# Residual rows through DRAM in place of TensorE, an MLP in groups of 256 rows, and a new order of steps

## The chip, the cores and the metric

One core of one Trainium2 chip runs the kernel. The metric is the device time of one execution in microseconds (us). The engines are TensorE (PE; its weight loads are PEld), VectorE (DVE), ScalarE (ACT), GpSimd (POOL) and SyncE (SP). POOL, SP and ACT issue DMAs.

## The reference

Inputs are q, k, v (4 batches, 8 heads, 768 rows, 64 columns, float32), `sort_net` (4, 8, 8, 8) and the MLP weights (512 x 2048 and 2048 x 512). In short:

```python
P = sinkhorn(sort_net)                 # 5 rounds of exp, row and column normalisation
k_sorted = einsum('bhij,bhjcd->bhicd', P, k_blocks)    # 8 blocks of 96 rows; v the same
attn = softmax(q_block @ k_sorted_block.T / 8)         # within each block
x = (attn @ v_sorted_block), heads side by side        # (4, 768, 512)
u = x + real(fft(fft(x, axis=1), axis=2))
un = (u - mean(u)) / sqrt(var(u) + 1e-6)               # over the 512 columns
out = u + relu(un @ w_ch1) @ w_ch2
```

## The kernel before

The program works batch by batch (b = 0 to 3 in the code, **batches 1 to 4** here), with two batches in flight: the attention of one batch overlaps the MLP of the one before. Nothing is left to a scheduler. The code declares some 1,300 steps (`step`, or `chain` for steps that follow each other), each with a name, a batch, the engines that may run it, what it reads and writes. `Plan.ORDER`, a long list of step numbers, gives the order in which they are issued, with a letter where an engine other than the first is taken. Each engine runs its own steps strictly in that order; a step that waits holds all behind it on its engine. Buffers come from rings of fixed size (`ring`), PSUM from eight banks.

Stages of a batch, with the step names that the prediction uses:

- `mix`: kron products of P (`make_kron`), mixed q, k, v on TensorE (`psQK`, `psV`), block means `a16`.
- attention: `psS` (scores), `max`, `exp`, `minus` (the exponentials less one, so that the means carry the constant part; in batches 3 and 4 in halves of four blocks, tile `es`), `turn_e` (transposed by a DMA on SP into `eT`), `psN` (values) and `norm`, which writes normalised values to `xr` (97 or 99 partitions, 8 blocks, 512 columns). The block means are kept apart and put into extra rows of `xr` by DMAs on SP (`a_out`, L634; `row_zero`, L642).
- Fourier transform: `fold`, `psWe`, `psWo` over the rows, `psF` over the columns, giving `PQ`.
- residual (`residual`): 6 tiles of 128 rows per batch, numbered by (i, m), i = 0 to 2, m = 0 or 1 for mirrored rows. A selection matrix `rsel` picks the 128 rows of x, in the order of the spectrum, out of `xr` on TensorE (L978; two matmuls of 512 columns, for i = 1 two of half the width). In batch 1 VectorE adds this to `PQ` straight from PSUM; in batches 2 to 4 it is copied to `u` (L431 on ACT, L435 on VectorE) and POOL adds `PQ` (`add_res`, L990, L991).
- normalisation: `stats` (L1005, L1006), `root` (L1014, L1015), `nm` (L1018), `normal` (L1028 on ACT, L1031 on VectorE), `transpose_u` (on SP by DMA, L1043; in batch 1 on TensorE).
- `mlp`: groups of three tiles (384 rows): 16 first-stage pieces of four matmuls (L1070) with a relu on ACT each (L1076), then 12 second-stage pieces of four matmuls (L1088), an evacuation on VectorE (L1097) into `outt`, and a store: an indirect scatter on POOL (L1109), for the last two tiles plain DMAs on SP and ACT (L1105).

POOL also issues the loads of k, q, v and weights (L443, L453, L1119, L1123). Most are throttled: POOL first copies one element of an earlier load (`landed`, L377), which waits until that has landed.

## Time and profile before

| | |
|---|---|
| median of 3 runs | 293.38 us (292.58 to 295.56) |
| profiled execution | 293.0 us, span 290.8 us, mean granted TensorE clock 0.992 |
| PE busy | 271.7 us (93%), 2581 matmuls |
| PEld, DVE, ACT, POOL busy | 160.5, 194.5, 175.2, 125.1 us |
| DMA | 30.40 MB, mean 105 GB/s |

The span runs from the first to the last instruction. Busy time is the sum of instruction durations on an engine. Matmuls overlap in TensorE's pipeline, so its busy time counts somewhat more than the pace at which it works through its queue.

### The profile page before, as it was taken

How to read it: one execution, taken by the hardware profiler on the slowest of the kernel's cores; microseconds unless marked ns; L12 is line 12 of the kernel's file. 1: busy time of each engine (PE TensorE's matmuls, PEld its weight loads, DVE VectorE, ACT ScalarE, POOL GpSimd, SP SyncE). 2: the span in 40 equal slices, each digit the busy share in tenths (PEclk: the TensorE clock that was granted, in tenths of full speed). 3: DMA queues.
4: the chain of work that ended last, by engine and by line, in shares of the span. 5: the costliest groups of instructions: out<-in, count | busy, mean ns of one | idle time of the engine just before them, and what ended most of it. 6: DMA issues, size and time to landing. Idle time of an engine off the chain costs nothing.

```text
span 290.8 us, 6800 instructions
## 1 busy us (share of the span) xinstructions
PE 271.7 (93%) x2581; PEld 160.5 (55%) x2581; DVE 194.5 (67%) x446; ACT 175.2 (60%) x444; POOL 125.1 (43%) x192
## 2 busy tenths in 40 slices
PE   6799899899969999979999899999999999999994
PEld 2466667556735566436656566455555555545541
DVE  6778989998868758657977887886575744211011
ACT  2268875878917776667775889969422660532520
POOL 8769596254527657689005117311010634211110
PEclk9989999999999999999999999999999999999999
DMA  7999949979964991895926622443310103312102
GB/s 100 182 217 192 184 66 180 215 114 139 151 95 70 140 152 41 145 160 113 136 54 126 134 60 66 103 108 92 79 37 18 38 18 109 78 42 80 38 36 72
DMA packets 50481, 30.40 MB, mean 105 GB/s; under 512 B 25851, under 2 KB 48587, under 8 KB 50448
## 3 DMA queue, kind: packets, MB, share of 16 engines
q0 software_dynamic: 19344, 20.48, 40.8%
q1 hardware_dynamic: 30906, 9.20, 16.2%
q8 instruction: 20, 0.33, 0.5%
q10 hardware_dynamic: 200, 0.30, 0.3%
q14 instruction: 11, 0.09, 0.1%
HBM read 28.50 MB, written 6.29 MB: 120 GB/s over the span
## 4 chain that ended last, share of the span: by engine, by line
PE 57%; DMA 19%; DVE 7%; ACT 6%; issue 4%; POOL 4%; SPq 0%; ACTq 0%; POOLq 0%; DVEq 0%
PE bank L1070 23%; PE bank L1088 20%; DMA w1sb<-in_moe_w_ch_dram 5%; DMA w2sb<-in_moe_w_ch_dram 5%; DMA unT<-un 4%; DMA eT<-es 4%; PE bank L978 2%; PE bank L935 2%; DMA v<-in_v_dram 2%; ACT sm L782 2%; ACT sm L770 1%; PE bank L873 1%; DVE mns L788 1%; PE bank L651 1%; POOL q L453 1%
## 5 line engine op out<-in xcount | busy, mean ns | idle before, releaser
L1070 PE MATMUL bank<-unT,w1sb 128*128 128x384 f16 x512 | 90.0, 326 | 3.6 <-DMA unT<-un 3.0
L1088 PE MATMUL bank<-w2sb,hr 128*128 128x512 f16 x384 | 88.0, 379 | 2.2 <-DMA w2sb<-in_moe_w_ch_dram 2.2
L1076 ACT ACTIVATE hr<-bank 128x384 f16<-128x384 f32 x128 | 56.5, 495 | 44.2 <-PE bank L1070 42.9
L1070 PEld LDWEIGHTS <-w1sb 128*128 128x128 f16 x512 | 48.3, 98 | 36.0 <-DMA unT<-un 3.8
L1088 PEld LDWEIGHTS <-hr 128*128 128x128 f16 x384 | 36.5, 98 | 42.9 <-issue 2.7
L1109 POOL DMA_INDIRECT out_dram<-outt,idx_sb x22 | 22.1, 1006 | 86.3 <-DVE outt L1097 61.0
L1097 DVE SCALAR_TENSOR_TENSOR outt<-u,bank 128x512 f32<-128x512 f32 x24 | 16.4, 682 | 41.8 <-PE bank L1088 35.6
L782 ACT ACTIVATE sm<-bank,mns 96x96 f32<-96x96 f32 x128 | 31.0, 348 | 6.5 <-DVE mns L788 6.4
L990 POOL TENSOR_TENSOR u<-u,PQ 128x257 f32<-128x257 f32 x18 | 12.3, 684 | 32.2 <-DVE PQ L948 25.5
L431 ACT CAST W<-bank 128x384 f16<-128x384 f32 (+1 forms) x36 | 11.8, 387 | 19.0 <-PE bank L895 9.8
L834 DVE TENSOR_TENSOR xr<-bank,rz 96x512 f16<-96x512 f32 x32 | 22.0, 687 | 1.1
L788 DVE TENSOR_REDUCE mns<-bank 96x8 f32<-96x768 f32 x16 | 14.9, 949 | 4.6 <-PE bank L743 4.1
L1005 DVE BATCH_NORM_STATS2 st<-u 128x6 f32<-128x512 f32 x24 | 16.4, 684 | 0.2
L753 DVE TENSOR_REDUCE mxs<-bank 96x8 f16<-96x768 f32 x16 | 14.8, 948 | 2.0 <-PE bank L743 2.0
L662 DVE SCALAR_TENSOR_TENSOR vo<-a,bank 128x384 f16<-128x384 f16 x24 | 12.6, 546 | 3.3 <-PE bank L651 2.9
L827 PEld LDWEIGHTS <-eT 97*128 97x128 f16 (+1 forms) x256 | 11.5, 101 | 5.8 <-DMA eT<-es 1.1
L827 PE MATMUL bank<-vs,eT 97*128 97x65 f16 (+1 forms) x256 | 12.9, 196 | 1.8 <-DMA eT<-es 0.5
L770 ACT ACTIVATE sm<-bank 96x768 f32<-96x768 f32 x16 | 12.9, 803 | 2.7 <-PE bank L743 1.8
L443 POOL DMA_DIRECT2D v<-in_v_dram x16 | 11.7, 730 | 3.9 <-PE bank L654 2.3
L873 PE MATMUL bank<-cso_sb,xso 120*128 120x384 f16 (+1 forms) x64 | 12.9, 326 | 0.2 <-DVE amt L599 0.2
L833 DVE RECIPROCAL rz<-bank 96x8 f32<-96x8 f32 x32 | 6.3, 197 | 9.8 <-PE bank L827 7.5
L798 ACT ACTIVATE es<-sm 96x384 f16<-96x384 f32 x21 | 11.1, 527 | 2.6 <-DMA eT<-es 1.3
(150 smaller groups left out, 425.4 us busy)
## 6 DMA issues: line engine op xcount, KB each, us to landing
vs<-vo SPq DMA_DIRECT2D x48, 65.0 KB
v<-in_v_dram POOLq DMA_DIRECT2D x16, 192.0 KB, 4.9
k<-in_k_dram POOLq DMA_DIRECT2D x15, 192.0 KB, 4.7
q<-in_q_dram POOLq DMA_DIRECT2D x15, 192.0 KB, 4.9
w1sb<-in_moe_w_ch_dram POOLq DMA_DIRECT2D x4, 512.0 KB, 10.2
w2sb<-in_moe_w_ch_dram POOLq DMA_DIRECT2D x4, 512.0 KB, 7.0
eT<-es SPq DMA_TRANSPOSE x32
cdh_sb<-cdh POOLq DMA_DIRECT2D x1, 387.0 KB, 4.1
```

Source lines behind the costliest of these rows:

```text
L770: ("exp", b, {"A": 810}, lambda e: nc.scalar.activation(sms[n].t.rearrange("p (t j) c -> p t (j c)", t=2), pS.t[0:BLK, :, 0:4 * BLK], AF.Exp),
L782: nc.scalar.activation(sm.t[:, i], pair(pS, BLK)[:, t, i % 4], AF.Exp, bias=mn.t[:, i:i + 1], scale=-1.0)
L788: ("max", b, {"V": 945}, lambda e: nc.vector.tensor_reduce(mn.t.rearrange("p (t j) -> p t j", t=2), pair(pS, BLK), axis=AX.X, op=ALU.min), ...
L827: nc.tensor.matmul(ps[0:wide(i).stop - BLK * i, i // 4, i % 4], et[0:97, wide(i)], vs[b % 2][:, 4 * y + i % 4, (D + 1) * h:(D + 1) * (h + 1)])
L834: nc.vector.tensor_tensor(xr2[b % 2][0:BLK, 4 * y:4 * y + 4, 128 * hp:128 * hp + 128].rearrange("p j (t d) -> p t j d", t=2), ps[:, :, :, ...
L873: nc.tensor.matmul(ps, x[0:n, j], cso[0:n, j, :], start=(j == 0), stop=(j == 3))
L1005: nc.vector.bn_stats(st.t, us[b, i, m].t)
L1070: nc.tensor.matmul(ps, w1sb[:, mc, 128 * fc:128 * fc + 128], unT[b, gr].t[:, mc, :], start=(mc == 0), stop=(mc == 3))
L1076: nc.scalar.activation(dst, bank(pH, [128, 384]), AF.Relu)
L1088: nc.tensor.matmul(ps, hr[f4].t[:, fc % 4, 128 * t:128 * (t + 1)], w2sb[:, fc, :], start=(fc == 0), stop=(fc == 15))
L1097: step("outt", b, {"V": 687}, lambda e, u=u, pC=pC, o=o: nc.vector.scalar_tensor_tensor(o.t, u.t, RSC, bank(pC, [128, DM]), op0=ALU.mult, ...
L1109: step("store", b, {"G": 1050}, lambda e: nc.gpsimd.indirect_dma_start(out=out.rearrange("b s m -> (b s) m"), out_offset=bass.IndirectOffs ...
```

## The change

In batches 2 to 4 the residual rows no longer pass TensorE. Two DRAM buffers `xd` of 768 rows by 512 columns in float16 take turns. SP first fills one with the block means, repeated (`fill`, new L993). Once all normalised values of a batch stand in `xr`, POOL adds them onto it with one accumulating DMA (`spill`, new L999). Then for each of the 6 tiles POOL gathers 128 rows by index into `xg` (`gather`, new L1006; the index has six columns more) and adds `PQ` to them, giving `u` (`add`, L988, L989). The residual matmuls, the copies of `u`, `a_out` and `row_zero` go for these batches; batch 1 keeps them.

The MLP works on groups of two tiles (one i, 256 rows). A first-stage piece is eight matmuls of 256 columns into one bank with one relu; a batch has 24 of them (32 before) and 24 second-stage pieces as before. The output is evacuated into `u` itself, so `outt` goes. Buffers: three `hr` of [128, 8, 256], three `unT` of [128, 4, 256], three `xg`. POOL may now take the halves of `minus` and the normalisation `un`. Six more warming matmuls stand in the Sinkhorn part, and `ORDER` is new throughout.

```diff
-    idx = np.concatenate([tok + S * b for b in range(B)], 1)
+    kept = NB * np.argsort(PERM)[tok % BLK] + tok // BLK
+    idx = np.concatenate([tok + S * b for b in range(B)] + [kept], 1)
...
     ORDER = """
-        0 39 1 2 3 8 9 28 29A 12 19 15 5 41 4 40V 37 38A 7 6 42V 10V 169V 53 54A 51 52A 26 81 27A 11 88 89 13 16 95 96
+        14 16 15 0 1 8 39 2 3 4 9 40V 10V 168G 28 29A 37 38A 26 27A 5 53 54A 6 7 57 55 13 11 58A 56A 51 52V 59 60 88
...
-    ring("hr", 4, [128, 4, 384], F16)
+    ring("hr", 3, [128, 8, 256], F16)
...
-    ring("unT", 2, [128, 4, 384], F16)
-    ring("outt", 2, [128, DM], F32)
+    ring("unT", 3, [128, 4, 256], F16)
+    ring("xg", 3, [128, DM], F16)
...
+    rows = ctx.enter_context(tc.tile_pool(name="rows", bufs=1, space=bass.MemoryType.DRAM))
+    xd2 = [rows.tile([S, DM], F16, name=f"xd{i}") for i in range(2)]
...
-            step("minus", b, {"V": 385, "A": 518}, g, r=[(sm, t)], w=[es])
+            step("minus", b, {"V": 360, "A": 520, "G": 850}, g, r=[(sm, t)], w=[es])
...
-            ("u", b, {"A": 585, "V": 685}, lambda e: copy(e, us[b, i, m].t, bank(pR, [128, DM])),
-             [pR], [us[b, i, m]]) if b else
             ("u", b, {"V": 730}, lambda e: add(e, us[b, i, m].t, bank(pR, [128, DM]), PQ[b, i], m),
...
-        step("add", b, {"G": 1340}, lambda e: add(e, u.t, u.t, pq, m), r=[(pq, 0), (pq, 1), u], w=[u])
+    def means_out(b):
+        xd = xd2[b % 2]
+        step("fill", b, {"S": 650}, lambda e: nc.sync.dma_start(
+            xd.rearrange("(g p) m -> p g m", g=G), a16[:, None, :].broadcast_to([128, G, DM])),
+            r=["a16"], w=[("xd", b % 2)], work=2000, hop=1600)
+
+    def rows_out(b):
+        xd, xr = xd2[b % 2], xr2[b % 2]
+        step("spill", b, {"G": 950}, lambda e: nc.gpsimd.dma_start(
+            xd.rearrange("(k i) m -> k (i m)", i=NB), xr[0:BLK].rearrange("k i m -> k (i m)"),
+            max_dma_last_dim=4096, accum_op=ALU.add),
+            r=[("x", b % 2, h, y) for h in range(H) for y in range(2)], w=[("xd", b % 2)], work=2500, hop=2200)
+
+    def rows_in(b, i, m):
+        us[b, i, m], pq, xg, t = Buf("u"), PQ[b, i], Buf("xg"), 6 * B + TILE[i, m]
+        step("gather", b, {"G": 1050}, lambda e: nc.gpsimd.indirect_dma_start(
+            out=xg.t, out_offset=None, in_=xd2[b % 2],
+            in_offset=bass.IndirectOffsetOnAxis(ap=idx[:, t:t + 1], axis=0)),
+            r=[("xd", b % 2), "idx"], w=[xg], work=500, hop=1500)
+        step("add", b, {"G": 1340}, lambda e: add(e, us[b, i, m].t, xg.t, pq, m),
+             r=[(pq, 0), (pq, 1), xg], w=[us[b, i, m]])
...
-        step("un", b, {"V": 545, "A": 814}, f,
+        step("un", b, {"V": 545, "A": 814, "G": 1130}, f,
...
+    def mlp(b, i):
+        h = [Buf("hr") for _ in range(2)]
+        MLP = 1e6 + 1e4 * b + 3e3 * i
+        for y in range(8):
             pH = Buf("bank")
...
+            def f(e, y=y, pH=pH):
+                ps = bank(pH, [128, 2, 256])
+                for x in range(2):
+                    fc = 2 * y + x
+                    for mc in range(4):
+                        nc.tensor.matmul(ps[:, x], w1sb[:, mc, 128 * fc:128 * fc + 128],
+                                         unT[b, i].t[:, mc, :], start=(x == 0 and mc == 0), stop=(mc == 3),
+                                         skip_group_check=True)
...
+            step("outt", b, {"V": 687}, lambda e, u=u, pC=pC: nc.vector.scalar_tensor_tensor(
+                u.t, u.t, RSC, bank(pC, [128, DM]), op0=ALU.mult, op1=ALU.add),
+                [pC, u], [u], prio=MLP - 1e8)
...
-            warm(7)
+            warm(12)
...
-    warm(2)
+    warm(3)
...
-        for gr in range(2):
-            mlp(b, gr)
+        for i in range(3):
+            mlp(b, i)
```

The order of instructions on an engine can be printed from the programs; a row is a line, the operation, output and inputs with buffer numbers, and the output's shape. On POOL before the change, where the last residual tile of batch 3 and the first of batch 4 get their `PQ` added, with stores between them:

```order
L1109 DMA out_dram<-outt_142,idx_sb 3072x512
L990 TENSOR_TENSOR u_117<-u_117,PQ_115 128x257
L991 TENSOR_TENSOR u_117<-u_117,PQ_115 128x255
L1109 DMA out_dram<-outt_143,idx_sb 3072x512
L1109 DMA out_dram<-outt_142,idx_sb 3072x512 x2
L990 TENSOR_TENSOR u_122<-u_122,PQ_114 128x257
L991 TENSOR_TENSOR u_122<-u_122,PQ_114 128x255
```

And on POOL of the changed kernel, from the spill of batch 4 on (L999 the spill, L1006 gathers, L1117 stores of earlier batches, L988 and L989 adds, L1045 a normalisation):

```order
L999 DMA xd_189<-xr_185 96x2x2048
L1006 DMA xg_144<-xd_189,idx_sb 128x512
L1117 DMA out_dram<-u_116,idx_sb 3072x512
L1006 DMA xg_143<-xd_189,idx_sb 128x512
L1117 DMA out_dram<-u_120,idx_sb 3072x512
L988 TENSOR_TENSOR u_122<-xg_144,PQ_113 128x257
L989 TENSOR_TENSOR u_122<-xg_144,PQ_113 128x255
L988 TENSOR_TENSOR u_116<-xg_143,PQ_113 128x257
L989 TENSOR_TENSOR u_116<-xg_143,PQ_113 128x255
L1006 DMA xg_142<-xd_189,idx_sb 128x512
L1117 DMA out_dram<-u_118,idx_sb 3072x512
L1006 DMA xg_144<-xd_189,idx_sb 128x512
```

An add needed only PSUM copies before; now it stands behind a gather, which stands behind the spill, with stores between them.

In batch 2 the same chain stands among the throttled loads. POOL of the changed kernel there, from the third gather on (L374 the `landed` copies, L451 and L441 loads):

```order
L1006 DMA xg_144<-xd_189,idx_sb 128x512
L374 COPY landed<-k_71 1x1
L451 DMA q_73<-in_q_dram 128x2x384
L988 TENSOR_TENSOR u_121<-xg_142,PQ_113 128x257
L989 TENSOR_TENSOR u_121<-xg_142,PQ_113 128x255
L374 COPY landed<-k_70 1x1
L441 DMA v_79<-in_v_dram 128x2x384
L1006 DMA xg_142<-xd_189,idx_sb 128x512
```

Between spill and third add there are loads that each wait for an earlier one; before, adds and loads also shared this queue, but no gather.

On TensorE, between the transforms of batch 4 (L895) and second-stage pieces of the MLP (L1088), before the change (L978 the residual matmuls):

```order
L1088 LDWEIGHTS hr_66
L1088 MATMUL bank<-w2sb,hr_66 128x512
L978 LDWEIGHTS rsel_sb
L978 MATMUL bank<-xr_184,rsel_sb 128x512
L978 LDWEIGHTS rsel_sb
L978 MATMUL bank<-xr_184,rsel_sb 128x512
L895 LDWEIGHTS xse
L895 MATMUL bank<-cse_sb,xse 128x194
```

And in the changed kernel, at the end of the same transforms, where the second-stage pieces (now L1100) follow at once:

```order
L895 LDWEIGHTS xse
L895 MATMUL bank<-cse_sb,xse 128x192
L895 LDWEIGHTS xse
L895 MATMUL bank<-cse_sb,xse 128x192
L1100 LDWEIGHTS hr_66
L1100 MATMUL bank<-w2sb,hr_66 128x512
```

The residual matmuls are out of the queue. From the last values of batch 4 to its first MLP matmul, TensorE of the changed kernel has 14 second-stage and 12 first-stage pieces of batch 3 (the latter of eight matmuls), and the transforms of batch 4 but for the last `psF`; for batch 3 and batch 2 some more of the like (29.2 and 37.5 us of pieces at the pace that the prediction derives).

194 lines of the change are left out of this document (89 added, 105 removed), and 3 rows, old and new, of the table ORDER.

## The prediction

> **What bounds the kernel now.** First the page's totals and its chain that ended last (shares of the span), then the table by stage (start:end, length, busy time and instruction counts of PE, PEld, DVE, ACT and POOL, granted clock, DMA share, GB/s).
>
> ```profile
> span 290.8 us, 6800 instructions
> PE 271.7 (93%) x2581; PEld 160.5 (55%) x2581; DVE 194.5 (67%) x446; ACT 175.2 (60%) x444; POOL 125.1 (43%) x192
> PE 57%; DMA 19%; DVE 7%; ACT 6%; issue 4%; POOL 4%; SPq 0%; ACTq 0%; POOLq 0%; DVEq 0%
> 40.00:60.00 20.00, 18.28 (x267) 12.84 (x265) 19.66 (x46) 14.32 (x29) 10.59 (x14) 1.00 1.12 178
> 100.00:120.00 20.00, 20.00 (x181) 12.13 (x180) 13.94 (x30) 15.23 (x38) 13.08 (x21) 1.00 0.70 113
> 200.00:220.00 20.00, 19.92 (x140) 11.26 (x139) 13.60 (x36) 7.78 (x21) 0.97 (x1) 1.00 0.24 54
> 240.00:260.00 20.00, 20.00 (x110) 10.58 (x109) 5.72 (x12) 7.38 (x19) 5.63 (x8) 1.00 0.28 80
> ```
>
> From 100 us on TensorE never rests for long and the other engines have room: what is taken from its queue there comes off the end. Between 40 and 60 us VectorE is 98% busy and DMA is loaded throughout: there TensorE waits for others now and then. Its waits, by its timeline, with the releaser behind the arrow:
>
> ```profile
> 12.08 0.27 PE L1193 MATMUL bank<-ident,pw 32*64 32x32 f32 x2 [1.62 <-DVE pw L1163]
> 57.62 0.61 PE L1052 MATMUL bank<-ident,un 128*128 128x128 f16 x8 [1.15 <-DVE qT L435]
> 85.73 1.02 PE L1088 MATMUL bank<-w2sb,hr 128*128 128x512 f16 x4 [1.25 <-DMA w2sb<-in_moe_w_ch_dram]
> 129.90 0.34 PE L1070 MATMUL bank<-unT,w1sb 128*128 128x384 f16 x1 [2.10 <-DMA unT<-un]
> 162.63 0.82 PE L1070 MATMUL bank<-unT,w1sb 128*128 128x384 f16 x4 [0.91 <-DMA unT<-un]
> ```
>
> The last two are the start of an MLP that waits for transposed rows, 3.0 us together. The changed part lies just ahead of those rows, so this is the wait to watch.
>
> **The change part by part.** TensorE first. The chain's pieces (start, length, line, matmuls) give the pace of one queue position better than the busy column, which counts the pipeline's overlap twice:
>
> ```profile
> 103.83 0.43 PE bank L978 x2
> 171.05 0.55 PE bank L978 x4
> 112.02 1.30 PE bank L1070 x8
> 180.44 0.86 PE bank L1088 x4
> 213.47 0.34 PE bank L895 x4
> 136.96 0.43 PE bank L827 x8
> ```
>
> *Residual matmuls.* Of 24 residual tiles 18 go: 12 with two full matmuls, 0.43 us each, and 6 with two half-width ones, about 0.25 (half of 0.55, less the drain of the last): 12 x 0.43 + 6 x 0.25 = 6.7 us less.
>
> *MLP in groups of 256.* The second stage keeps its 384 matmuls. The first had 512 of 384 columns at 1.30/8 = 0.1625; it gets 768 of 256. From 0.1625 (384 columns) and 0.86/4 = 0.215 (512), a column costs 0.41 ns and a matmul 5 ns, so one of 256 costs 0.110: 768 x 0.110 - 512 x 0.1625 = 84.5 - 83.2, 1.3 us more at most; by 0.34/4 = 0.085 for 193 columns it is 0.111, the same. A weight load takes 98 ns in its own rows, near 110, but the L827 matmuls with their own weight loads follow each other every 0.43/8 = 0.054, so the loads stay covered. The fewer, larger relu instructions run beside this. I take 0.7, since the two lengths are read to 0.01 us. TensorE: **-6.0 us**.
>
> *The early part.* These copies and POOL's present work stand in the groups (busy, mean ns of one):
>
> ```profile
> L431 ACT COPY u<-bank 128x512 f32<-128x512 f32 x10 | 6.0, 597 | 2.0 <-PE bank L978 2.0
> L435 DVE COPY u<-bank 128x512 f32<-128x512 f32 x8 | 5.5, 685 | 3.1 <-PE bank L978 2.8
> L1031 DVE TENSOR_SCALAR un<-u,mv,rstd 128x512 f16<-128x512 f32 x14 | 7.6, 549 | 0.0
> L510 POOL TENSOR_TENSOR kron<-pcs,small_sb 128x512 f16<-128x512 f32 x4 | 4.3, 1085 | 6.1 <-PE bank L711 6.0
> L814 POOL TENSOR_SCALAR eT<-sm 96x768 f16<-96x768 f32 x1 | 2.1, 2132 | 3.7 <-ACT sm L770 3.7
> ```
>
> Both copies go, and the new order puts the two remaining kron products of the later batches, ten half-tiles of exp minus one and nine normalisations on POOL. VectorE loses 5.5 us of copies, and three normalisations of batch 1 (3 x 0.549 = 1.6) around the 40 to 60 us where it is full; waits such as the 1.15 us at 57.62 can shrink. The second-stage weights are issued ahead of most of batch 3's loads, so the 1.25 at 85.73 can go. At the head, five plus one more warming matmuls stand in the gap ahead of 12.08; they end before the data comes. That gap is followed by one stretch at half clock:
>
> ```profile
> 13.10:16.50 3.40, 3.40 (x36) 2.34 (x35) 2.75 (x6) 0.82 (x3) 1.48 (x2) 0.50 1.31 204
> ```
>
> If the filled gap keeps the clock, 1.7 us of TensorE time is saved. (The Trainium skill, "TensorE: Matmul & The Clock Gate", Part 1, asks for a wholly idle window of about 3.4 us before the clock halves; by it the extra matmuls gain nothing. The trace shows 0.50 behind a gap of 1.62 us, so the row goes against it here.) All of the early part: bounds +1.5 (more DMA in a loaded stretch) to -4.1 (1.7 + 1.15 + 1.25); I take **-1.5**, nearest to the clock row with its doubt.
>
> *POOL.* Added: 18 gathers and 3 spills at the 1.0 us of the indirect store, ten halves at 2.13/2 = 1.1, nine normalisations at 2.13 x 512/768 = 1.4, two kron products; less the one L814. 21 + 11 + 13 + 2 - 2 = 45 us, POOL goes from 125 to some 170 of 285. It is not the bound as a sum; its order counts, since a gather waits on POOL until the spill has landed, and behind it stand stores, adds, half-tiles and loads.
>
> *The new chain.* Per batch: normalised values, spill, gathers, adds, statistics, root, normalisation, transposes, first MLP matmul. The residual matmuls needed no transfer in this place. Its links:
>
> ```profile
> L834 DVE TENSOR_TENSOR xr<-bank,rz 96x512 f16<-96x512 f32 x32 | 22.0, 687 | 1.1
> L1109 POOL DMA_INDIRECT out_dram<-outt,idx_sb x22 | 22.1, 1006 | 86.3 <-DVE outt L1097 61.0
> L990 POOL TENSOR_TENSOR u<-u,PQ 128x257 f32<-128x257 f32 x18 | 12.3, 684 | 32.2 <-DVE PQ L948 25.5
> L1005 DVE BATCH_NORM_STATS2 st<-u 128x6 f32<-128x512 f32 x24 | 16.4, 684 | 0.2
> L1006 DVE BATCH_NORM_AGGREGATE mv<-st 128x2 f32<-128x6 f32 x24 | 4.4, 182 | 0.8
> L1014 ACT ACTIVATE rstd<-mv,epst 128x2 f32<-128x2 f32 x12 | 3.5, 295 | 3.5 <-DVE mv L1006 3.0 <-DVE nm L1018 0.3
> L1015 ACT ACTIVATE rstd<-rstd 128x2 f32<-128x2 f32 x12 | 2.4, 204 | 0.4
> 124.25 5.61 DMA unT<-un
> ```
>
> And of the DMA issues, with KB each and the median us from issue to landing:
>
> ```profile
> q<-in_q_dram POOLq DMA_DIRECT2D x15, 192.0 KB, 4.9
> w2sb<-in_moe_w_ch_dram POOLq DMA_DIRECT2D x4, 512.0 KB, 7.0
> out_dram<-outt,idx_sb POOLq DMA_INDIRECT x22, 3.0
> ```
>
> For batch 4, X being the spill's landing: 0.9 (values with their reciprocal) + 1.0 (spill's issue) + X, then on POOL gather, store, gather (3.0), the gather's landing 3.0 (as the indirect store's), the second add 1.4 (two halves of 0.68), then 0.9, 0.5, 0.2 for the bias, 1.4 (the normalisation that is on POOL) and 5.6: 17.9 + X. On TensorE between the last values of batch 4 and its first MLP matmul stand 14 second-stage pieces of batch 3 (14 x 0.86 = 12.0), 12 first-stage pieces of eight matmuls (12 x 0.88 = 10.6) and 3.5 of transforms: 26.1. **The wait is nothing up to X = 8.2.** For batch 3 the same count gives 19.2 + X (one half-tile, one store and one gather more, less overlap) against 29.2: 10.0. For batch 2 the cover is 37.5, but POOL has ten loads of later batches, each ahead of a gather or an add and most of them held until an earlier load has landed; 31 + X, so 6.5.
>
> X stands in no row. It is 768 KB from SBUF, added onto as much in DRAM. Below: 3.0, the store of 256 KB. From 192 to 512 KB the landing grows by 2.1, so 768 KB would take 8.7, and with DRAM read as well as written, twice the bytes, some 14. The weight rows were taken at a DMA share around 1; in batches 3 and 4 it is 0.24 to 0.7. I take 8, near the 512 KB row: no wait in batches 3 and 4, 1.5 in batch 2, and 4 for loads, fills (768 KB each on SP's queue, ahead of transposes) and stores that come late; less the 3.0 that the same place costs now: **+2.5**. (The Trainium skill, "DMA: Bandwidth & Descriptors", Anatomy of one DMA, fits a transfer on this path as 2.0 us plus bytes at 436 GB/s; X would be 3.8, the 1.5 in batch 2 would go and the time be 286.5. It gives 2.5 for the 192 KB load that took 4.9, so the rows decide.)
>
> Unchanged: the tail. Behind the last matmul the same two tiles leave by SP and ACT, the third by POOL.
>
> **Sum.** -6.0 - 1.5 + 2.5 = -5.0. The profiled execution took 293.0 us, 2.2 around its span; 293.0 - 5.0 = **288.0**. The median shown, 293.4, is 0.4 above it, so this is 1.8% below the median. A change of 1%, 2.9 us, is about what a measurement of this kernel can tell from none; runs shown lie from 292.6 to 295.6.
>
> **Rivals.**
> 1. *The spill is late: slower.* Place: POOL's gather behind the spill, three times. From X = 6.5, 8.2 and 10.0 each further us comes three times. At X = 14 the waits are 7.5 + 5.8 + 4.0 = 17.3 in place of 1.5: 288.0 + 15.8 = 303.8; at 12, 11.3: 297.8. It turns slower than before above X = 10.5. For: an add in DRAM has no row, and batch 2's falls where DMA share is 0.7. Against: the DMA engines are three quarters idle at batch 4.
> 2. *The loads hold POOL in batch 2.* The gathers change places with loads that are throttled by landing; 3 MB more (fill, spill with its read-back, gathers) pass there: 17 us of DMA at the 178 GB/s of the full stage, and of the 38 us of cover, at a DMA share of 0.70, some 11 are free. That is 4 to 6 us late, 292 to 294: within 1%.
> 3. *Everything is covered.* X is 5 or less, the early waits go: -6.0 - 4.1 + 1.0 = 283.9.
> 4. *Short matmuls pay for their weight loads.* If 256 columns cost 0.125 instead of 0.110, 768 x 0.015 = 11.5 more, 299.5. The L895 and L827 pieces speak against it.
>
> **How the numbers follow.** Forecast 0.46 (its own range 285.5 to 290.4), rival 1 0.18, rival 2 0.18, rival 3 0.14, rival 4 0.04. Faster by over 1% holds the forecast and rival 3, 0.60; rival 2 is within 1%, 0.18; rivals 1 and 4 are slower, 0.22. The range leaves out the lower edge of rival 3 and the dearer half of rival 1 and most of 4: 283 to 298.
>
> **What would show it.** In the profile after: residual matmuls only 12 (batch 1); first-stage matmuls 768 at a pace of 0.11; the spill from issue to landing (8 or less); the wait of the first MLP matmul of batches 2, 3 and 4 for transposed rows, 1.5, 0 and 0; POOL near 170 us busy and its waits for the spill; clock 1.00 from 13 us on; VectorE below 95% at 40 to 60 us. The prediction is wrong if X is over 10, if TensorE waits for half-tiles that stand on POOL behind a gather, or if the last MLP starts later than its cover.

## The result: 8% slower, and the profile after

The changed kernel takes 318.6 us in the median (315.1 to 321.8), the kernel before 293.0 in the same session. The ratio is 1.0816, with a 95% interval of 1.0689 to 1.0944. In some executions the chip is in a slower state (the one of 321.8 here); every ratio leaves such executions out, which is why 1.0816 is less than 318.6 / 293.0 and why some kernels below have one time and no ratio. The forecast was 288.0, so even the sign was wrong. The profiled execution took 315.1 us, 22.1 more than the profiled one of before.

First the page of the changed kernel: span, totals, and the chain that ended last.

```profile
span 313.2 us, 7206 instructions
PE 271.2 (87%) x2805; PEld 184.2 (59%) x2805; DVE 191.0 (61%) x430; ACT 162.0 (52%) x390; POOL 181.8 (58%) x234
PE 44%; DMA 18%; DVE 12%; POOL 11%; issue 8%; ACT 2%; another core or an unknown queue 1%; ACTq 0%; SPq 0%; DVEq 0%; POOLq 0%
```

TensorE has as much busy time as before, in a span 22 us longer, and its share of the chain fell from 57% to 44%. Where the time lies shows in the table by stage (columns as in the prediction):

```profile
40.00:60.00 20.00, 19.13 (x279) 14.02 (x278) 18.61 (x47) 14.66 (x29) 13.26 (x16) 1.00 0.98 172
100.00:120.00 20.00, 17.88 (x164) 11.40 (x162) 12.04 (x28) 12.27 (x38) 16.67 (x22) 0.94 0.79 152
120.00:140.00 20.00, 17.52 (x138) 11.50 (x137) 10.15 (x21) 10.89 (x35) 12.96 (x19) 0.89 0.82 120
280.00:300.00 20.00, 8.94 (x61) 5.67 (x58) 1.29 (x2) 1.68 (x3) 4.88 (x5) 0.80 0.19 71
```

The stretch from 40 to 60 us became better (19.13 busy in place of 18.28), as forecast. From 100 to 120 TensorE was busy throughout before and is no longer, up to 140 its clock is below 1.00, and from 280 on every engine is idle for more than half of the time. TensorE's larger waits, from its timeline:

```profile
34.76 0.67 PE L827 MATMUL bank<-vs,eT 97*128 97x65 f16 x16 [1.45 <-DVE xse L850]
84.58 0.54 PE L895 MATMUL bank<-cse_sb,xse 120*128 120x194 f16 x4 [1.86 <-DVE xse L855]
116.43 0.20 PE L743 MATMUL bank<-kz,qT 64*128 64x96 f16 x1 [1.85 <-DVE vo L662]
134.03 0.42 PE L827 MATMUL bank<-vs,eT 97*128 97x65 f16 x8 [2.48 <-DMA vs<-vo]
183.69 0.32 PE L651 MATMUL bank<-v,kron 128*128 128x384 f16 x1 [2.58 <-DVE PQ L948]
301.94 4.91 PE L1100 MATMUL bank<-w2sb,hr 128*128 128x512 f16 x14 [13.00 <-ACT hr L1088]
```

The last row alone is 13.0 us: the last 14 matmuls of the program wait for relus (`hr`, L1088) on ScalarE. They then take 4.91 us, where 14 x 0.215 = 3.0 would do at full clock. ScalarE had its input long before (its own wait below is put down to `issue`, not to an engine); the row names it because it came last. What ScalarE stood behind is in POOL's timeline, the last stores (L1117, the indirect scatter into the output):

```profile
281.78 0.99 POOL L1117 DMA_INDIRECT out_dram<-u,idx_sb  x1 [18.91 <-DMA out_dram<-u]
285.37 0.97 POOL L1117 DMA_INDIRECT out_dram<-u,idx_sb  x1 [2.60 <-DMA out_dram<-u,idx_sb]
288.90 0.98 POOL L1117 DMA_INDIRECT out_dram<-u,idx_sb  x1 [2.55 <-DMA out_dram<-u,idx_sb]
294.12 0.97 POOL L1117 DMA_INDIRECT out_dram<-u,idx_sb  x1 [4.24 <-DMA out_dram<-u]
297.12 0.97 POOL L1117 DMA_INDIRECT out_dram<-u,idx_sb  x1 [2.03 <-DMA out_dram<-u,idx_sb]
303.07 0.97 POOL L1117 DMA_INDIRECT out_dram<-u,idx_sb  x1 [4.98 <-DMA out_dram<-u]
306.60 0.97 POOL L1117 DMA_INDIRECT out_dram<-u,idx_sb  x1 [2.56 <-DMA out_dram<-u,idx_sb]
```

Seven stores, and the releaser of each is the landing of another store into the output. The program tracks the output as one tensor, since the rows of a scatter are known only from the index; so each store waits until the one ahead of it in the program has landed. In a row they cost 1.0 us of issue and 2.0 to 2.6 us of waiting each. The direct stores of batch 4 (L1113, on SP and ACT) wait in the same chain, and POOL's wait for them (18.91, 4.24 and 4.98 above). ScalarE's two stand ahead of its last relus; they left at 300.19, and the relus followed. All waits of this kind together, from the list of waits (us in total, times, longest):

```profile
POOL out_dram L1117 <- DMA out_dram<-u: 28.1, 3, 18.9
POOL out_dram L1117 <- DMA out_dram<-u,idx_sb: 19.8, 8, 4.8
ACT hr L1088 <- issue: 17.7, 1, 17.7
```

Three of the seven (the first two and the sixth) carry rows of batches 2 and 3. VectorE finished the last of these near 253.7 us:

```profile
252.40 1.28 DVE L1105 SCALAR_TENSOR_TENSOR u<-u,bank 128x512 f32<-128x512 f32 x2 [0.58 <-PE bank L1100]
```

The kernel before could not put them off: its output rows went into `outt`, with two buffers, so the third row needed the first store done. The change writes them into `u`, with ten buffers, and the new order uses that room. The last scatters of the kernel before stood apart, but for one pair:

```profile
266.79 0.96 POOL L1109 DMA_INDIRECT out_dram<-outt,idx_sb  x1 [5.83 <-DVE outt L1097]
269.78 0.96 POOL L1109 DMA_INDIRECT out_dram<-outt,idx_sb  x1 [2.02 <-DMA out_dram<-outt,idx_sb]
280.65 0.96 POOL L1109 DMA_INDIRECT out_dram<-outt,idx_sb  x1 [9.91 <-DVE outt L1097]
```

### The profile page after: what moved, and what is told of

It is laid out like the page before. It is cut to its first block, busy times and chain, and to the rows that moved or that the text cites. A ratio compares the mean times of both kernels' runs of the same rounds, so it can differ in the third digit from the quotient of the medians.

```text
span 313.2 us, 7206 instructions
## 1 busy us (share of the span) xinstructions
PE 271.2 (87%) x2805; PEld 184.2 (59%) x2805; DVE 191.0 (61%) x430; ACT 162.0 (52%) x390; POOL 181.8 (58%) x234
## 4 chain that ended last, share of the span: by engine, by line
PE 44%; DMA 18%; DVE 12%; POOL 11%; issue 8%; ACT 2%; another core or an unknown queue 1%; ACTq 0%; SPq 0%; DVEq 0%; POOLq 0%
PE bank L1100 16%; PE bank L1081 14%; DMA out_dram<-u,idx_sb 5%; DMA w2sb<-in_moe_w_ch_dram 3%; PE bank L873 2%; DMA eT<-es 2%; PE bank L827 2%; POOL un L1045 2%; DMA unT<-un 2%; DMA xd<-xr 2%; DVE st L1019 2%; PE bank L743 2%; PE bank L651 2%; POOL xg L1006 2%; DMA q<-in_q_dram 1%
## 5 line engine op out<-in xcount | busy, mean ns | idle before, releaser
L1100 PE MATMUL bank<-w2sb,hr 128*128 128x512 f16 x384 | 93.8, 389 | 16.0 <-ACT hr L1088 16.0
L1081 PE MATMUL bank<-unT,w1sb 128*128 128x256 f16 x768 | 93.9, 275 | 1.0 <-DMA unT<-un 0.7
L1088 ACT ACTIVATE hr<-bank 128x512 f16<-128x512 f32 x96 | 54.2, 600 | 70.2 <-PE bank L1081 50.2
L1081 PEld LDWEIGHTS <-w1sb 128*128 128x128 f16 x768 | 74.1, 99 | 16.3 <-DMA unT<-un 0.9
L1100 PEld LDWEIGHTS <-hr 128*128 128x128 f16 x384 | 36.8, 100 | 55.5 <-ACT hr L1088 18.1
L1117 POOL DMA_INDIRECT out_dram<-u,idx_sb x22 | 22.2, 1011 | 58.1 <-DMA out_dram<-u 28.1
L1105 DVE SCALAR_TENSOR_TENSOR u<-u,bank 128x512 f32<-128x512 f32 x24 | 16.1, 682 | 41.5 <-PE bank L1100 41.5
L1006 POOL DMA_INDIRECT xg<-xd,idx_sb x18 | 18.4, 1023 | 18.1 <-DMA xd<-xr 11.2
L1045 POOL TENSOR_SCALAR un<-u,mv,rstd 128x512 f16<-128x512 f32 x9 | 19.6, 2181 | 7.7 <-ACT rstd L1029 7.6
L800 POOL TENSOR_SCALAR es<-sm 96x384 f16<-96x384 f32 x7 | 9.1, 1300 | 13.3 <-ACT sm L782 5.4
L948 DVE TENSOR_TENSOR PQ<-bank,ot 128x258 f32<-128x258 f32 x24 | 9.3, 419 | 8.5 <-ACT ot L429 3.3
L451 POOL DMA_DIRECT2D q<-in_q_dram x15 | 11.1, 740 | 5.3 <-PE bank L690 5.0
```

The costliest lines, as they stand in the source:

```text
L1006: step("gather", b, {"G": 1050}, lambda e: nc.gpsimd.indirect_dma_start(out=xg.t, out_offset=None, in_=xd2[b % 2], in_offset=bass.Indirect ...
L1045: plan.engines[e].tensor_scalar(o, x, scalar1=mv[b, i].t[:, m, 0:1], scalar2=rstd[b, i].t[:, m:m + 1], op0=ALU.subtract, op1=ALU.mult)
L1081: nc.tensor.matmul(ps[:, x], w1sb[:, mc, 128 * fc:128 * fc + 128], unT[b, i].t[:, mc, :], start=(x == 0 and mc == 0), stop=(mc == 3), skip ...
L1088: nc.scalar.activation(dst, bank(pH, [128, 2, 256]), AF.Relu)
L1100: nc.tensor.matmul(ps, h[fc // 8].t[:, fc % 8, 128 * m:128 * (m + 1)], w2sb[:, fc, :], start=(fc == 0), stop=(fc == 15))
L1105: step("outt", b, {"V": 687}, lambda e, u=u, pC=pC: nc.vector.scalar_tensor_tensor(u.t, u.t, RSC, bank(pC, [128, DM]), op0=ALU.mult, op1=A ...
```

## The experiments

**Theory:** the late stores carry most of the loss. **Rivals:** GpSimd is too loaded as a whole; the way through DRAM is too long; the early part and the other small waits. Steps are named by their numbers in `ORDER`; a letter behind a number is the engine. Ratios are to the kernel before on the same chip.

### Stores early

```diff
 # ORDER: 361, 617, 651 are stores of batches 1 and 2; 925 to 959 of batch 3; 1138 to 1176 of batch 4
-... 1100 1124 1133 1122 1107 1129 ... 1128 959 617 953 1108 1106 1109 ...
+... 1100 1124 1133 1122 1107 925 953 1129 ... 1128 1108 1106 959 931 1109 ...
-... 1151 1167 1143 1156 ... 1171 1176 1182 ... 931 1189 651 ... 1144 ... 1173 1175 925 1188 ...
+... 1151 1167 1143 1144 1156 ... 1171 1176 1175 1173 1182 ... 1189 ... 1188 ...
```

(617 and 651 now stand ahead of batch 4's spill, 361 ahead of a half-tile near 200 us.)

> The changed kernel with only its stores into the output moved: the three old ones of batches 1 and 2 that stood among the last 90 us go to places where GpSimd idles between 195 and 218 us, those of batch 3 go behind the last gathers, and of batch 4 each stands next to the addition that completes its rows; the two that ScalarE issues stand ahead of the indirect ones that come later. Nothing is left out and no other step is moved. Theory (the stores wait for one another, about 3.3 us each, and hold the last relus through ScalarE): the 13.0 us wait ahead of the last 14 matmuls goes, these run at full clock (3.0 in place of 4.9 us), at most four GpSimd stores are left behind 270 us, and the time is 298 to 302 us. Rival 1 (GpSimd is too loaded as a whole): the same rows on the same engine, 311 us or more. Rival 2 (the new chain through DRAM and the other small waits of TensorE carry the loss): 308 us or more.

Measured: 304.5 us, ratio 1.0405 (1.0317 to 1.0493). The end, from TensorE's and POOL's timelines of this kernel:

```profile
285.36 7.93 PE L1101 MATMUL bank<-w2sb,hr 128*128 128x512 f16 x36
287.94 0.97 POOL L1118 DMA_INDIRECT out_dram<-u,idx_sb  x1 [15.22 <-DVE u L1106]
291.45 0.97 POOL L1118 DMA_INDIRECT out_dram<-u,idx_sb  x1 [2.54 <-DMA out_dram<-u,idx_sb]
294.96 0.97 POOL L1118 DMA_INDIRECT out_dram<-u,idx_sb  x1 [2.54 <-DMA out_dram<-u,idx_sb]
```

The last 36 matmuls run through. Both rivals' bounds, 308 and 311 us, are missed on the low side: moving nothing but stores gives back half of the loss, 4.1 of 8.2 points (12 us). That is 2.5 to 6.5 us short of what the theory asked (298 to 302 us), and three stores are still in a row at the end.

### ScalarE freed, the chain of stores kept

```diff
-                step("store", b, {"SA"[y % 2]: 400}, ...
+                step("store", b, {"S" if i == 1 else "SA"[y % 2]: 400}, ...
 # and in ORDER
-... 1199 1200 1173 1175 925 ...
+... 1199 1200 1173S 1175S 925 ...
```

> The changed kernel with the two direct stores that ScalarE issues for the fifth tile of batch 4 put on SyncE's queue, at the same place in the order; nothing else. Theory (a chain of stores): the 13.0 us wait of TensorE goes, since ScalarE reaches its last relus, but the seven GpSimd stores behind 280 us still follow each other and the last rows leave behind them: 312 to 317 us, at most 3 less than the changed kernel. Rival (it is ScalarE's place alone that costs, the stores overlap): 300 to 304 us.

Measured: 314.5 us, ratio 1.0718 (1.0605 to 1.0831). TensorE's end, and the first and the last of POOL's seven late stores:

```profile
282.64 7.93 PE L1100 MATMUL bank<-w2sb,hr 128*128 128x512 f16 x36
280.41 0.98 POOL L1117 DMA_INDIRECT out_dram<-u,idx_sb  x1 [18.92 <-DMA out_dram<-u]
304.75 0.97 POOL L1117 DMA_INDIRECT out_dram<-u,idx_sb  x1 [2.56 <-DMA out_dram<-u,idx_sb]
```

The largest wait in TensorE's timeline is gone, and the time hardly moves (313.3 us in place of 315.1 in the profiled executions; the intervals overlap): the seven stores take the same 24 to 25 us, and the program ends with them. So 13.0 us of TensorE's waiting were worth some 2 us by themselves; they lay beside the chain of stores.

### Work taken off GpSimd

```diff
 # 13 steps: un of batches 2 to 4, minus of batches 3 and 4
-... 550G ... 966G ... 1081G ...
+... 550V ... 966V ... 1081V ...
```

> The changed kernel with 13 steps taken off GpSimd and put on VectorE: six normalisations of batches 2 to 4 (2.2 us each on GpSimd) and seven half-tiles of exp minus one of batches 3 and 4 (1.3 each), 22 us of GpSimd's work; the stores stay where they are. Theory (late stores): within 4 us of the changed kernel, 311 to 318 us. Rival (GpSimd's load as a whole): 8 us less or more, 307 us or below.

Measured: 324.3 us, ratio 1.1054 (1.0925 to 1.1182), so it is slower still, which neither side had expected. POOL's busy time fell from 181.8 to 158.9 us. So taking load off GpSimd does not help while the stores stand where they are: the seven late ones go out within 25 us of each other as before, only 8 us later. On VectorE the moved steps wait for their inputs (it stands idle for 10.7 us ahead of its half-tiles, 2.1 in the changed kernel) with others behind them, which can explain the loss; the mean clock is lower too (0.933, 0.955 in the changed kernel), and no run separates the two.

### The kernel before, with stores put late

```diff
-    ring("u", 10, [128, DM], F32)
+    ring("u", 12, [128, DM], F32)
...
-                o = Buf("outt")
...
-                    o.t, u.t, RSC, bank(pC, [128, DM]), op0=ALU.mult, op1=ALU.add),
-                    [pC, u], [o], prio=MLP - 1e8)
+                    u.t, u.t, RSC, bank(pC, [128, DM]), op0=ALU.mult, op1=ALU.add),
+                    [pC, u], [u], prio=MLP - 1e8)
 # and in ORDER
+... 1281 969 1007 1019 1013 1226 1270 ...
```

> The kernel before, with the output rows written in place of their residual rows as the change does it (so that a store may wait), and four stores of batch 3 moved behind the second store of batch 4, ahead of the last two; no other part of the change. Theory: four stores in a row cost 3.0 to 3.5 us each, the last two GpSimd stores go out near 283 and 286 us and the direct ones behind them near 290: 5 to 8 us longer than before, 298 to 301 us. Rival (a store costs GpSimd its 1.0 us of issue and the landings overlap): within 1 us of the kernel before.

Measured: 296.8 us, ratio 1.0115 (1.0021 to 1.0208). The second of the four late stores on POOL, and the next but two:

```profile
274.31 0.96 POOL L1107 DMA_INDIRECT out_dram<-u,idx_sb  x1 [2.06 <-DMA out_dram<-u,idx_sb]
283.25 0.96 POOL L1107 DMA_INDIRECT out_dram<-u,idx_sb  x1 [2.02 <-DMA out_dram<-u,idx_sb]
```

They go out every 3.0 us, and the last store in the row at 286.75. The price in time, 3.7 us, is below the 5 to 8 expected; a store in a row costs 3.0 here, the low end. Of the 4.2 us by which the span grows, 3.0 lie behind the last matmul (7.3 us in place of 4.3); the other 1.2 come from earlier, and this profile has a lower clock long before the stores that were moved (0.83 from 20 to 40 us, in place of 1.00). So a row of late stores lengthens the end with no more of the change than output rows that stay in `u`.

### The end in another order

```diff
-... 1132 1135 1136 1155 ... 1165 1166 1137 1138 1180 1193 1194 1199 1200 1188 1195 1190 1192 1196 1197 ...
+... 1132 1135 1136 1137 1138 1155 ... 1165 1166 1180 1193 1194 1188 1195 1190 1192 1196 1199 1200 1197 ...
```

> The kernel with its stores early (304.5 us) with the end put in another order: the addition and the store of batch 4's mirrored first tile stand behind its last matmuls (some 20 us sooner), and the mirrored third tile ends four pieces ahead of the third tile instead of two. Theory: three GpSimd stores 3.5 us apart held the last direct ones until 297.9 us, 4.5 us behind the last matmul; now one is left ahead of them, and the span ends 4 to 5 us behind the last matmul instead of 8.2: 300 to 302 us. Rival (the last rows' own landing takes that long, whatever goes ahead of them): 304 us or more.

Measured: 300.8 us, ratio 1.0229 (1.0185 to 1.0272). The span now ends 4.7 us behind the last matmul (8.2 with stores early alone, 4.3 in the kernel before). With this the end is repaired: 8.2% have become 2.3%. What follows is about the rest, some 7 us over the kernel before although TensorE has less to do.

### Waits in batches 2 and 3

A sum of values on GpSimd beside VectorE's folds:

```diff
-... 20 517 458 ... 437 467 438 415 369 ... 320 378 558 ...
+... 20 517 458 ... 437 438 415 369 ... 320 378 467 558 ...
```

> The kernel with its stores early (304.5 us) with one GpSimd sum of batch 3's values (three additions, 2.1 us) moved from behind batch 2's spill, where VectorE folds batch 2's rows, to behind the first gather. Theory: VectorE's two fold additions took 2.27 us beside that sum where the same pair takes 0.49 us elsewhere, and TensorE waited 2.0 us for them at 85.7 us and then ran at 0.91 of its clock in that stretch: they take 0.6 us, the wait falls below 0.6, the stretch from 80 to 100 us has a clock of 1.00, and the time is 301 to 303 us. Rival (the folds are slow for another reason, such as the spill's reading of the same rows): the pair still takes 2 us, 304 us or more.

Measured: 301.8 us in one execution. VectorE's pair of folds with GpSimd's sum beside it (the kernel with stores early), and then without it (this one):

```profile
85.58 2.27 DVE L856 TENSOR_TENSOR xse<-xs 96x256 f16<-96x256 f16 x2
86.14 1.34 POOL L464 TENSOR_TENSOR vh<-v 128x384 f32<-128x384 f16 x1
```

```profile
82.00 0.49 DVE L856 TENSOR_TENSOR xse<-xs 96x256 f16<-96x256 f16 x2
```

The spill runs beside the folds in both, so it isn't the spill: the sum on GpSimd holds VectorE. (The Trainium skill, "SBUF — State Buffer", section "SBUF: two separate sides", says that the two share a pair of ports that one instruction locks as a whole, also against a VectorE operation with two SBUF inputs. The rows agree: 2.27 against 0.49 us.) TensorE's wait of 2.0 us there fell to 0.24. Some 20 us later stands a wait of 2.13 for ScalarE's exponentials that the kernel with stores early did not have; the time is still within what the theory gave (301 to 303 us), by one execution.

The store ahead of batch 3's spill:

```diff
-... 689V 339 367 714 ... 966G 967 825 791A ... 976G ...
+... 689V 339 714 ... 966G 967 825 367 791A ... 976G ...
```

> The kernel with its stores early (304.5 us) with one more store moved: the second of two that stood in a row ahead of batch 3's spill now goes behind the spill and the half-tile that follows it. Theory: in the profile of the kernel with early stores that second store waited 4.6 us for the landing of the first, with the spill (769 KB) behind it on GpSimd; the gathers came late, the additions came late, and the two PQ buffers that the additions read were not free, so that TensorE stood 3.9 us at 182.4 us. The spill goes out about 4 us sooner, the 3.9 us wait falls below 1, the time is 300.5 to 302.5 us. Rival (the way through DRAM is too long by itself, wherever the spill stands): TensorE still waits 2.5 us or more there, 303.5 us or more.

(The store stands right behind the spill, ahead of the half-tile 976.) Measured: 304.4 us in one execution. The spill went out only 1.8 us sooner (168.02 against 169.77), since it then waits for the values. The wait near 183 us fell from 3.87 to 1.86, but a wait of 3.45 for transposed rows appeared at 200.6. By the time, the rival is right. All these moves at once, with the mixed values of batch 3's last head ahead:

> All moves together: stores early, the store behind the spill, the sum away from the folds, the new end, and one VectorE copy of mixed values (batch 3's last head) ahead of three output additions and two maxima, for which TensorE waited 2.8 us at 134 us through a move of rows. The computation is the changed kernel's. Theory (order, not work): the gains of the parts add up, 4 + 2 + 3.5 + 2, to 292 to 295 us, level with the kernel before. Rival (the waits fill up elsewhere, GpSimd being loaded): 298 us or more.

Measured: 302.7 us, ratio 1.0310 (1.0245 to 1.0375); the gains don't add up, and the kernel with only the stores and the new end moved is no slower. Next, from that kernel, without the store behind the spill, and with VectorE's statistics behind what they held up:

```diff
-... 437 467 438 ... 309 522 ... 676 528 346 ... 678V ... 541 544 354 ... 489 ... 495 ... 545 ... 491 493 ... 311 505 702 ... 728 509 510 ... 836 ... 979 ...
+... 437 438 ... 309 467 522 ... 676 346 ... 678V 528 ... 541 354 ... 489 ... 495 ... 491 493 544 545 ... 311 505 509 702 ... 728 510 ... 979 836 ...
```

> The kernel with early stores and the new end (300.8 us) with three more kinds of moves, nothing else: the sum of batch 3's values stands behind the folds and ahead of the first gather, where GpSimd waits for the spill anyway; VectorE's four statistics of batches 2 and 3 that waited for GpSimd's additions (3.1 us at 181.7, 2.5 at 115.0) stand behind the maxima, mixed values and copies that they held up; and the last head's mixed values of batch 3 stand ahead of the output additions. Theory (what is left over the kernel before is order: an engine that waits for GpSimd with others' work behind it): the fold pair takes 0.5 us, the waits of TensorE for folds (2.0), for moved rows (3.2) and the stretch at 0.91 of the clock shrink: 294 to 297.5 us. Rival (the chain through GpSimd itself is as long as TensorE's work in these stages): 299 us or more.

Measured: 300.3 us, ratio 1.0217 (1.0080 to 1.0354), no gain over the kernel with the new end (1.0229), as the rival had it. From here on "the kernel with all moves" means this one. Then a third PQ buffer:

```diff
-    ring("W", 6, [128, 2, 385], F16)
-    ring("PQ", 2, [128, 2, LT, 2], F32)
+    ring("W", 5, [128, 2, 385], F16)
+    ring("PQ", 3, [128, 2, LT, 2], F32)
```

> The same with three PQ buffers in place of two (and five W buffers in place of six, for the room). Theory: TensorE's wait near 183 us (3.0 us, released by ScalarE's patch of PQ) comes from the two PQ buffers, which the additions behind the late gathers still hold; with a third it falls below 0.5 and the time by 1.5 to 3 us against the kernel without it. Rival (ScalarE is late by itself, behind its exponentials): the wait stays above 1.5 us and the time within 1 us.

Measured: 300.9 us in one execution. TensorE's wait without and with the third buffer (timelines of the two kernels), and the piece of the second kernel's chain just ahead of it (start, length, what):

```profile
184.82 0.42 PE L828 MATMUL bank<-vs,eT 97*128 97x65 f16 x8 [3.05 <-ACT PQ L966]
```

```profile
185.24 0.62 PE L828 MATMUL bank<-vs,eT 97*128 97x65 f16 x8 [3.99 <-ACT PQ L966]
175.87 5.46 DMA eT<-es
```

The theory fell: with a free PQ buffer ScalarE is just as late, behind half-tiles that wait for a transpose of 5.46 us. This is where the way through DRAM loads the transfers: from 160 to 180 us the DMA share is 1.03 in the changed kernel and 0.39 before. Leaving the spill out tests that:

```diff
-        step("spill", b, {"G": 950}, lambda e: nc.gpsimd.dma_start(
-            xd.rearrange("(k i) m -> k (i m)", i=NB), xr[0:BLK].rearrange("k i m -> k (i m)"),
-            max_dma_last_dim=4096, accum_op=ALU.add),
+        step("spill", b, {"G": 950}, lambda e: None,
```

> The kernel with early stores and the new end (300.8 us) without the three spills: the normalised values are not added into DRAM, so that the gathers read the block means alone and wait only for the fill. 2.4 MB of DMA and three GpSimd issues are gone. Theory A (the spill's landing of about 8 us holds GpSimd and, through additions, PQ buffers and statistics, TensorE): the waits of GpSimd for the spill (11 us in two places) go, that of TensorE near 183 us falls below 1, the time is 295 to 298 us. Rival B (GpSimd's order and its slow normalisations make the waits, whatever the spill takes): 299.5 us or more.

Measured: 296.5 us, ratio 1.0111 (1.0002 to 1.0220). TensorE passes the place without a wait:

```profile
178.76 0.42 PE L828 MATMUL bank<-vs,eT 97*128 97x65 f16 x8
```

ScalarE's half-tiles ahead of that place waited 0.6 and 1.8 us for transposes with the spill and don't wait without it, while the DMA share from 160 to 180 us falls from 1.07 to 0.64. The span falls by 4.3 us (294.6 against 298.9), the ratio by 1.2 points, 3.5 us; the two intervals just overlap, so the size is uncertain. Is it the adding?

```diff
-            max_dma_last_dim=4096, accum_op=ALU.add),
+            max_dma_last_dim=4096),
```

> The kernel with early stores and the new end (300.8 us), whose three spills write their 768 KB over the block means in DRAM instead of adding onto them, so that the means are missing from the residual rows. Bounds of the prediction for the landing: 8.7 us for 768 KB written once, some 14 with DRAM read as well; it took 8.1 in the median. If the adding costs as much again, a plain write lands in 4 to 5 us, and the time falls by 2 us or more; if the bytes or the descriptors set it, the landing stays at 7 us or more and the time within 1.5 us.

Measured: 302.2 us, ratio 1.0239 (1.0111 to 1.0367). POOL waits for the last spill in both kernels; from its issue to the gather behind it (adding, then plain):

```profile
221.69 1.22 POOL L1000 DMA_DIRECT2D xd<-xr  x1 [0.59 <-DVE xr L835]
230.58 1.07 POOL L1007 DMA_INDIRECT xg<-xd,idx_sb  x1 [7.67 <-DMA xd<-xr]
```

```profile
220.96 0.73 POOL L1000 DMA_DIRECT2D xd<-xr  x1 [0.46 <-issue]
227.47 1.04 POOL L1007 DMA_INDIRECT xg<-xd,idx_sb  x1 [5.77 <-DMA xd<-xr]
```

That is 8.9 against 6.5 us: adding costs 2.4 of the 8.9, between the two expectations, and the time doesn't show it (1.0239 against 1.0229).

The first part of the change undone, all the rest kept:

```diff
-        step("gather", b, {"G": 1050}, ...
-        step("add", b, {"G": 1340}, lambda e: add(e, us[b, i, m].t, xg.t, pq, m), ...
+        step("psR", b, {"V": 730}, f, ...)   # the residual matmuls into a bank, then VectorE's add from it
...
-        if b:
-            rows_out(b)
-        else:
-            row_zero(b)
+        row_zero(b)
```

> The order of the kernel with all moves (298.2 to 304.6 us, span 297.7 in its profile), with the change's first part undone: the residual rows of batches 2 to 4 come from TensorE again, at the place of each addition, which VectorE makes straight out of PSUM. No fill, no spill, no gather; the groups of 256 rows, the new order and the half-tiles on GpSimd stay. TensorE has 6.7 us more of work, VectorE some 13 us (18 x 0.73), GpSimd some 45 less. Theory (the way through DRAM makes the waits of batches 2 and 3, by the spill's landing and by what stands behind it): the waits near 183 and 195 us go and the time is 292 to 297 us, not above the kernel with all moves although TensorE works more. Rival (what is left is the order of the rest): 6.7 us of work come on top, 303 us or more.

Measured: 303.5 us, ratio 1.0238 (1.0145 to 1.0331); the span of the profile is 302.4. (One attention step of batch 3, scores, moved by four places in the order, to find a free bank.) In microseconds this is the rival's number: 4.7 us of span come on top of the kernel with all moves (297.7) for 6.7 us of work. But the kernel before ran slower on this chip as well, and by the ratios the two stand level (1.0238 and 1.0217). The waits near 183 and 195 shrink to 1.0 and less, while TensorE now waits 5.5 us in all for VectorE's additions, which this version puts there. So the theory's 292 to 297 us did not come; how much of the rest the way through DRAM makes, this run leaves open.

### The clock

The warming matmuls of the change, alone, in the kernel before:

```diff
-            warm(7)
+            warm(12)
...
-    warm(2)
+    warm(3)
```

> The kernel before with one part of the change alone: twelve and three warming matmuls at the head in place of seven and two. The forecast held that the gap of 1.6 us at 12 us costs a stretch of 3.4 us at half clock, 1.7 us: then the clock from 0 to 20 us is 1.00 in place of 0.91 and the time falls by 1.2 to 1.7 us. Rival (the stretch at half clock comes at the next wait instead): a later stretch below 1.00, and the time within 0.8 us of before.

Measured: 295.3 us, ratio 1.0062 (1.0017 to 1.0108). The clock at the place rose from 0.72 to 1.00 (12 to 18 us, first the kernel before):

```profile
12.00:18.00 6.00, 5.92 (x65) 4.16 (x66) 4.27 (x10) 2.25 (x5) 2.42 (x4) 0.72 1.30 206
```

```profile
12.00:18.00 6.00, 6.00 (x91) 4.07 (x90) 3.93 (x10) 2.67 (x7) 2.95 (x5) 1.00 1.31 210
```

Nothing is gained: the matmuls of the Sinkhorn part's end start at 13.11 in place of 12.08, behind the fillers, and the stretches from 40 to 80 us are at 0.96 (1.00 before). Filling waits in the middle of the kernel with all moves is another matter:

```diff
 # 1228 to 1235, 1208: idle matmuls, two or four each
+... 103 1228 1229 1208 133 ... 1230 1231 672 ... 1235 761 ... 1232 1233 1234 978 ...
```

> The kernel with all moves (298 to 300 us; granted clock 0.973) with idle matmuls on constant data put where its profile shows TensorE waiting: 10 ahead of the wait of 2.61 us at 37.2, 8 ahead of 2.03 at 135.4, 4 ahead of 1.27 at 163.6 and 12 ahead of 3.05 us at 184.8, each 0.215 us, so each group a little shorter than its wait; they feed nothing. Theory (a wait of TensorE is paid twice, once itself and once by the 3.4 us at half clock behind it, 1.7 us): the stretches below 1.00 behind these places go, the mean clock rises above 0.98, the time falls by 2 to 4 us. Rival (what is waited for sets the pace of these stages, so a faster TensorE only waits longer at the next place): the clock rises and the time stays within 1 us.

Measured: 296.8 us, ratio 1.0147 (1.0086 to 1.0208). Mean clock and the 5 us behind the largest wait, without the fillers and with them:

```profile
core 0: 297.7 us, clock 0.973
184.80:189.80 5.00, 4.98 (x31) 3.07 (x32) 2.60 (x7) 3.62 (x12) 3.89 (x6) 0.66 0.46 118
```

```profile
core 0: 292.1 us, clock 0.994
180.40:185.40 5.00, 5.00 (x56) 3.78 (x55) 3.09 (x9) 3.20 (x10) 3.49 (x4) 1.00 0.48 130
```

The profiled spans differ by 5.6 us, the ratios by 0.7 points, 2 us, with overlapping intervals. The clock came back; that the time came with it is likely and not shown by the ratios. This is the best complete version of the changed kernel that was found, still above the kernel before. Two normalisations of batch 2 moved to VectorE on top of it:

```diff
-... 550G ... 564G ...
+... 550V ... 564V ...
```

> The same with two normalisations of batch 2 (2.1 to 2.4 us each on GpSimd) on VectorE, where one takes 0.55 us. Theory (the chain through GpSimd sets batch 2's stage: half-tile, normalisation, additions, statistics, mixed values): TensorE's waits between 115 and 136 us shrink by another 1 to 2 us, and so does the time. Rival (VectorE, waiting in its own order for the root, holds others up by as much): no change or slower.

Measured: 300.4 us, ratio 1.0297 (1.0217 to 1.0376), slower, as its rival had it.

## Why the prediction was wrong

**The step that failed is "Unchanged: the tail."** The prediction counted the stores as POOL's 1.0 us of issue each and looked at who leaves last, not at when the rows of earlier batches leave. It saw stores among gathers and adds, and in its +2.5 put 4 us for "loads, fills ... and stores that come late" together, without asking what a store waits for. The kernel before has the row, in its list of waits:

```profile
POOL out_dram L1109 <- DMA out_dram<-outt,idx_sb: 5.2, 3, 2.4
```

Three stores that waited for the store ahead of them, 5.2 us in all: harmless while stores are apart, 3.0 to 3.5 us each in a row of seven. Repairing it took the ratio from 1.0816 to 1.0405 (stores) and 1.0229 (end), 5.9 points or 17 us, where the prediction had nothing for the tail and at most those 4 us for late stores. No rival had this mechanism.

The other steps:

- *TensorE, -6.0: by count and pace the work fell as forecast.* Of the residual matmuls only the 12 of batch 1 are left. A first-stage matmul goes at 0.109 us, by a piece of the chain of the changed kernel:

```profile
269.41 2.62 PE bank L1081 x24
```

  So rival 4 (0.125) is out. What failed is "what is taken from its queue there comes off the end": that holds only where TensorE sets the pace, and from 100 to 140 us it no longer does (17.88 and 17.52 of 20 us busy).
- *The early part, -1.5: mis-sized, nothing.* The filled gap at the head keeps its clock and gains no time (ratio 1.0062 in the kernel before): the fillers do not "end before the data comes", they start the next matmuls 1.0 us late. In the changed kernel a stretch at 0.66 follows the wait of 1.45 at 34.76 instead, and the wait for the second-stage weights that went is followed by one of 1.86 for the folds.
- *The new chain, +2.5: the link was right, the place wrong.* X was taken as 8 and is 8.1 (DMA issues of the kernel with the new end: KB each, median us to landing):

```profile
xd<-xr POOLq DMA_DIRECT2D x3, 768.0 KB, 8.1
```

  The Trainium skill's fit ("DMA: Bandwidth & Descriptors", Anatomy of one DMA) gave 3.8; the measurement decides. The first MLP matmuls wait 0.7 us in all, so rivals 1 and 2 are out at their place. That is partly luck: TensorE came there late from its other waits, which lengthens the cover; without the spill, where it comes sooner, its first-stage matmuls wait 5.9 us for transposed rows. The spill still costs 3.5 to 4.3 us, by the rows through transposes and ScalarE's half-tiles ahead of the MLP, a path that the prediction had not followed.
- *POOL, 170 us: 182.* A normalisation takes 2.18 us there, not 1.4, a half-tile 1.30, not 1.1, and three of the "ten half-tiles" are whole tiles of 2.14 us:

```profile
L1045 POOL TENSOR_SCALAR un<-u,mv,rstd 128x512 f16<-128x512 f32 x9 | 19.6, 2181 | 7.7 <-ACT rstd L1029 7.6
```

  Scaling by columns from the 96x768 row did not hold for 128 partitions and two operands per partition. It is not the cause by itself: putting work elsewhere made the kernel slower.
- *"Clock 1.00 from 13 us on": wrong.* The mean is 0.955, before 0.992.

What stays open: with the end repaired the kernel is 2.2% over the kernel before (1.5% with the waits filled). Leaving the spill out took 1.2 points off, filling the waits 0.7, each with overlapping intervals, and undoing the whole DRAM way left the ratio where it was. What else makes up the remainder is not shown; the order of batches 2 and 3 is a guess that no run here takes apart.

## What to carry to other kernels

For every store, look up what it waits for, not only what it costs to issue: here scatters into one tensor formed a chain, and rows that may stay longer in their buffers let a new order push that chain to the end, where nothing covers it. Time taken off the busiest engine counts only in stages where that engine is never waiting; where others feed it, a wait removed can show up at the next feed, as several did here. A wait that the profile shows on the critical engine can be worth next to nothing (13.0 us here, for 1.8 us of the profiled time), if a chain that doesn't pass that engine ends last anyway.

## What was unexpected of the hardware

- Behind some of TensorE's waits the granted clock falls, behind others of the same length it doesn't. It stood at 0.50 over 3.4 us in the prediction's row; 0.66 over 5 us, as below, is what 3.4 us at half clock would give. In the changed kernel, the stretches behind the waits of 1.45, 2.48 and 2.58 us:

```profile
34.70:39.70 5.00, 4.94 (x52) 3.28 (x53) 3.54 (x10) 2.30 (x8) 1.43 (x3) 0.66 0.89 177
134.00:137.40 3.40, 3.37 (x27) 2.56 (x28) 0.89 (x2) 0.00 (x0) 3.06 (x7) 0.62 1.04 127
183.70:188.70 5.00, 4.47 (x44) 3.13 (x44) 4.25 (x9) 3.81 (x14) 3.65 (x5) 1.00 0.28 57
```

  (The Trainium skill, "TensorE: Matmul & The Clock Gate", Part 1, describes a free-running window of 3.4 us that has to be idle. Free-running fits that equal waits fare differently; that waits of 1.45 to 3.05 us suffice does not fit a window idle throughout.) With idle matmuls in four waits the clock was 1.00 behind each; behind two of them (2.03 and 1.27 us) it had been 1.00 without.
- A GpSimd addition of 1.34 us made two VectorE additions in float16 take 2.27 us in place of 0.49.
- A spill of 768 KB that adds in DRAM took 8.9 us from issue to the gather it releases, one that only writes 6.5.
